# Two-round loops on TensorE in a load-bound decode kernel

## Chip, cores, metric

One core of one Trainium2 chip. The metric is device time in microseconds, the median of several runs; "span" is the time from the first to the last instruction in the profiled run, 1.7 us less than that run's time. Every run quoted as a comparison is fast (on one core: not more than 1.5% above the fastest run of the same kernel), except where it is said.

## The reference, cut to what matters

```python
x  = A_x                                   # 4 x 1 x 512
xn = layernorm(x)
q  = (xn @ wq)                             # 32 heads of 128; 8 KV heads, window of 1024 keys
p  = softmax(q @ k.T / sqrt(128));  o = p @ v
s  = o @ wo                                # wo: 4096 x 512
h  = gelu(layernorm(xn) @ w1 + b1)         # 512 x 1792
g  = silu(h @ w2 + b2)                     # 1792 x 512
return x + s * g
```

All is bfloat16. Four tokens meet 28.85 MB of weights and cache, so each byte is used by very little arithmetic.

## The kernel before

A recording layer keeps the operations of each engine in program order and derives the semaphore waits. Each of the eight K groups (1 MB) is transposed in four tiles of eight matmuls, copied by VectorE, and used for scores; each V group goes into 32 matmuls plus one for the softmax denominators. Everything is written out: 1089 matmuls on TensorE. There are eight 1 MB buffers, so a V load waits for the transposes of the K group whose buffer it takes.

```python
def T(n):                                  # transposes of tile n, then VectorE's copy
    ...
    t = add("pe", fn, d_k[g], c_id, cp.get(n - NB), ...)       # eight pe.transpose into psK
    cp[n] = add("dve", lambda e: e.tensor_copy(kt_buf[:, n % NKT, :], psK[n % NB][:, 0:1024]),
                t, sc.get(n - NKT))
...
for n in range(LAG, NUN + LAG):            # all 8 groups x 4 tiles, LAG = 8
    if n < NUN: T(n)
    S(n - LAG)                             # scores; exp on ScalarE after every fourth
load_v(0); d_w1 = ...; load_v(1); d_w2 = ...
for g in range(HKV):
    if g >= 2: load_v(g)
    if g == 4: d_wox = ...                 # last 128 rows of wo: 60 + 60 + 8 KB, outer dimension 3, 3 and 8
    PV(g)
    if g == 0: epilogue(0); mlp1()
    if g >= 2: epilogue(g - 1)
    if g == 1: mlp2(); mlp3()              # second layer: 56 matmuls of 4 columns, and b2
    if g == 2: mlp4()
epilogue(HKV - 1)
rows = to_rows()                           # all groups, after the last epilogue
wo(... wox ...); wo(... groups 0-6 ...); wo(... group 7 ...)
```

The result is then multiplied by the gate, transposed, added to x and stored.

The softmax here doesn't subtract the row's maximum and nothing guards it: scores larger than these inputs give would overflow.

## Time and profile before

| kernel before | |
|---|---|
| time, median of 3 (range) | 76.81 us (76.61 to 76.92) |
| span | 75.0 us |
| last completion of the last load | 71.89 us |
| packets on TensorE's instruction queue | 8 of 16 KB |

The prediction below shows the lines. One kind of record needs a word: the trace has, for each load, when each of its parts completed. A load over all sixteen DMA engines has sixteen parts (sixteen completion records), and a consumer waits for the last one: the last part of the last load comes at 71.89 us and the four matmuls that read it start at 71.94. The wox loads, with outer dimensions 3, 3 and 8, end in 3, 3 and 8 parts. "The parts" below are always those of the very last load, a quarter of wo's last group, in us from the start of the span. They say how far the sixteen engines had come when the stream of loads ended.

### The profile page before, as it was taken

The page shows a single profiled execution, that of the slowest core. Times are in us where ns is not written, and L with a number is a line of the kernel's source. Part 1 is how long each engine was busy: PE and PEld are TensorE (multiplying, and loading weights), DVE is VectorE, ACT ScalarE, POOL GpSimd, SP SyncE. Part 2 cuts the span into 40 slices and gives each one's busy share as a digit, 9 for nine tenths or more (in the row PEclk, how much of TensorE's full clock was granted, in tenths as well). Part 3 has the DMA queues.
Part 4 walks back from the last instruction along what each step waited for, and adds up shares of the span by engine and source line. Part 5 has one row for each costly group of instructions (what it writes and reads, how often), then busy time and mean ns, then how long its engine had stood idle before and what let it go on. Part 6 is the DMA issues. An engine that isn't in the chain of part 4 may idle for free.

```text
span 75.0 us, 2384 instructions
## 1 busy us (share of the span) xinstructions
PE 49.1 (66%) x1089; PEld 40.3 (54%) x1089; DVE 41.2 (55%) x84; ACT 9.7 (13%) x16; POOL 7.2 (10%) x19
## 2 busy tenths in 40 slices
PE   0000029965689999959979937910899977379670
PEld 0000029953279989959979902500886555268640
DVE  0778106894258989959977060269639774620020
ACT  0611000000270320303203600230000000000000
POOL 6999300000000000000000000000000000000000
PEclk9999999999999999999999995555555555555555
DMA  1999999998999999999999999999999999999800
GB/s 37 271 413 420 417 420 476 437 420 376 433 437 433 415 433 420 424 415 464 419 398 425 461 413 401 424 420 428 419 429 428 420 409 420 417 411 419 322 25 2
DMA packets 4266, 28.99 MB, mean 387 GB/s; under 512 B 508, under 2 KB 648, under 8 KB 1697
## 3 DMA queue, kind: packets, MB, share of 16 engines
q1 hardware_dynamic: 4206, 28.84, 92.6%
q8 instruction: 8, 0.13, 0.6%
q10 hardware_dynamic: 50, 0.01, 0.1%
q14 instruction: 2, 0.01, 0.0%
HBM read 28.85 MB, written 0.00 MB: 385 GB/s over the span
## 4 chain that ended last, share of the span: by engine, by line
DMA 39%; PE 34%; SPq 15%; DVE 5%; issue 3%
DMA wo_sb<-in_A_wo_dram 26%; PE psK L299 20%; SPq L510 14%; DMA kv_buf<-in_A_k_cache_dram 13%; PE psS L318 6%; DVE kt_buf L305 4%; PE psO L383 3%; PE psS L314 2%; PE psM L555 2%; DVE q_sb L389 1%; PE psK L395 1%; PE psK L367 1%; PE psS L576 1%; SPq L218 1%; SPq L211 0%
## 5 line engine op out<-in xcount | busy, mean ns | idle before, releaser
L299 PE MATMUL psK<-ident,kv_buf 128*128 128x128 bf16 x256 | 20.5, 231 | 11.9 <-DMA kv_buf<-in_A_k_cache_dram 10.7
L305 DVE COPY kt_buf<-psK 128x1024 bf16<-128x1024 bf16 x32 | 21.1, 691 | 7.4 <-PE psK L299 7.3
L299 PEld LDWEIGHTS psK<-ident,kv_buf 128*128 128x128 bf16 x256 | 16.3, 104 | 11.3 <-DMA kv_buf<-in_A_k_cache_dram 10.7
L318 PEld LDWEIGHTS psS<-qT,kt_buf 128*128 128x128 bf16 x256 | 9.4, 96 | 2.1 <-issue 1.2
L318 PE MATMUL psS<-qT,kt_buf 128*128 128x16 bf16 x256 | 10.4, 169 | 0.2 <-issue 0.2
L336 PEld LDWEIGHTS psO<-P_buf,kv_buf 128*128 128x128 bf16 x256 | 7.5, 103 | 3.4 <-DMA kv_buf<-in_A_v_cache_dram 1.8
L336 PE MATMUL psO<-P_buf,kv_buf 128*128 128x16 bf16 x256 | 8.0, 174 | 0.9 <-DVE den_sb L349 0.7
L349 DVE TENSOR_REDUCE den_sb<-psS 128x16 f32<-128x512 f32 x8 | 5.5, 687 | 5.1 <-PE psS L342 4.9
L326 ACT ACTIVATE P_buf<-psS 128x512 bf16<-128x512 f32 x8 | 4.8, 597 | 16.2 <-PE psS L318 16.2
L555 PE MATMUL psM<-OW,wo_sb 128*128 128x4 bf16 x124 | 4.1, 167 | 0.8 <-DMA wo_sb<-in_A_wo_dram 0.8
L342 PE MATMUL psS<-P_buf,ones_bf 128*128 128x512 bf16 x8 | 4.5, 561 | 0.0
L555 PEld LDWEIGHTS psM<-OW,wo_sb 128*128 128x128 bf16 x124 | 3.7, 105 | 1.1 <-DMA wo_sb<-in_A_wo_dram 0.9
L572 DVE TENSOR_TENSOR sg_sb<-psM,g_sb 128x16 f32<-128x16 f32 x1 | 0.2, 185 | 5.8 <-PE psM L555 5.8
L421 PE MATMUL psK<-w_sb,yT 128*32 128x448 bf16 x16 | 2.0, 561 | 1.8 <-issue 1.8
L314 PE MATMUL psS<-negm,ind 128*128 128x512 bf16 x8 | 3.0, 380 | 0.0
L449 PE MATMUL psM<-ident,b_sb 4*128 4x16 bf16 x1 | 0.2, 190 | 3.8 <-DVE hT L444 3.8
L431 DVE SCALAR_TENSOR_TENSOR kt_buf<-kt_buf,psK 128x448 f32<-128x448 f32 x1 | 0.6, 622 | 3.7 <-ACT kt_buf L430 3.7
L449 PEld LDWEIGHTS psM<-ident,b_sb 4*128 4x128 bf16 x1 | 0.1, 99 | 4.3 <-DVE hT L444 4.3
L390 ACT ACTIVATE q_sb<-psO 128x512 bf16<-128x512 f32 x1 | 0.6, 597 | 13.1 <-PE psO L383 13.1
L267 DVE CAST P_buf<-x_bf 4x512 f32<-4x512 bf16 x1 | 1.0, 956 | 2.2 <-DMA x_bf<-in_A_x_dram 2.2
L352 DVE RECIPROCAL rden<-den_sb 128x16 f32<-128x16 f32 x8 | 2.0, 253 | 0.3
L440 DVE TENSOR_TENSOR kt_buf<-kt_buf,psK 128x448 bf16<-128x448 f32 x1 | 2.1, 2083 | 0.0
(74 smaller groups left out, 36.0 us busy)
## 6 DMA issues: line engine op xcount, KB each, us to landing
kv_buf<-in_A_k_cache_dram SPq DMA_DIRECT2D x8, 1024.0 KB, 20.6
kv_buf<-in_A_v_cache_dram SPq DMA_DIRECT2D x8, 1024.0 KB, 24.0
wq_sb<-in_A_wq_dram SPq DMA_DIRECT2D x2, 2048.0 KB, 11.4
w_sb<-in_B_w_dram SPq DMA_DIRECT2D x2, 1792.0 KB, 28.3
wo_sb<-in_A_wo_dram SPq DMA_DIRECT2D x3, 1024.0 KB, 24.0
wo_sb<-in_A_wo_dram SPq DMA_DIRECT2D x1, 512.0 KB, 19.6
wo_sb<-in_A_wo_dram SPq DMA_DIRECT2D x1, 256.0 KB, 16.4
wo_sb<-in_A_wo_dram SPq DMA_DIRECT2D x1, 128.0 KB, 14.6
```

The lines of the kernel that those rows point to most:

```text
L299: last = pe.transpose(psK[n % NB][:, j * 128:(j + 1) * 128], kv_buf[:, g, u * UT + j, :], ident[:, :])
L305: cp[n] = add("dve", lambda e: e.tensor_copy(kt_buf[:, n % NKT, :], psK[n % NB][:, 0:1024]), t, sc.get(n - NKT))
L314: pe.matmul(psS[g % 2][:, 0:512], ind[:, :], negm[:, :], start=True, stop=False, skip_group_check=True)
L318: last = pe.matmul(psS[g % 2][:, c * 16:(c + 1) * 16], kt_buf[:, n % NKT, j * 128:(j + 1) * 128], qT[:, g * 16:(g + 1) * 16], start=False, ...
L326: ex[g] = add("act", lambda e: e.activation(P_buf[:, g, :], psS[g % 2][:, 0:512], AF.Exp, scale=SCALE), sc[n])
L336: last = pe.matmul(pso[:, 0:16], kv_buf[:, (HKV + g) % NS, c, :], P_buf[:, g, c * 16:(c + 1) * 16], start=(c == 0), stop=(c == NC - 1))
L342: den[g] = add("pe", lambda pe: pe.matmul(psS[g % 2][:, 0:512], ones_bf[:, :], P_buf[:, g, :], start=True, stop=True), ex[HKV - 2 + g % 2] ...
L349: v = add("dve", lambda e: e.tensor_reduce(den_sb[:, cs], bass.AP(psS[g % 2], 0, [[512, 128], [1, 16], [16, NC]]), AX.X, ALU.add), den[g])
L383: last = pe.matmul(psO[m // 4][32 * s:32 * s + 32, 0:512], xT[:, c, :], wq_sb[:, c, m * 512:(m + 1) * 512], start=(c == 0), stop=(c == 3), ...
L440: v = add("dve", lambda e: e.tensor_tensor(bass.AP(kt_buf, 4 * UT * 128, [[NKT * UT * 128, 128], [1, 32], [32, FC]]), f32k(3).rearrange("p ...
L510: d_wo.append((g0, g1, i0, i1, pg.dma("sp", "wo%d" % n, lambda e: e.dma_start(wo_sb[:, g0:g1, i0:i1, :], wo_r[:, g0:g1, i0:i1, :]))))
L555: last = pe.matmul(psM[:, PS_W + c * 4:PS_W + (c + 1) * 4], w[:, c * 128:(c + 1) * 128], o, start=(st and c == 0), stop=sp, skip_group_che ...
```

## The change

Its intent is to halve TensorE's program: K groups 0-3 and 4-7 run through the same instructions, and so do V groups 0-3 and 4-7. For that, both rounds must name the same buffers (hence qR, the one tile from which both rounds read their queries, and the copies of P, the softmax weights), semaphores are lowered again in the loop, and the second MLP layer stands in a branch taken in the first V round only, in a form with fewer instructions. The rows of groups 0 to 6 are made ahead of the last epilogue, and wox, the load of the last 128 rows of wo, becomes two loads with outer dimensions 5 and 3. The queries are now made before the first transposes, and the scores follow the transposes by 3 tiles and no longer by 8. Cut to its core:

```diff
     def emit_pe(self, pe):
+                with pe.Fori(0, 2, 1) as i:
+                    ...                    # all operations of the first round, waits valid for both
+                    if first:
+                        with pe.If(i < 1):
+                            ...            # the second MLP layer
+                    for name, (s, step) in mine.items():
+                        pe.sem_inc(s, -step)
...
-    d_wq = [load_wq(0)]; load_k(0); load_k(1); d_wq.append(load_wq(1)); load_k(2..7)
+    d_wq = [load_wq(0), load_wq(1)]; load_k(0..3)
...
-            kv_buf[:, (HKV + g) % NS, :, :], ...), t_last[(HKV + g) % NS]
+            kv_buf[:, NG + g % NG, :, :], ...), pv_op[g - NG] if g >= NG else None
...
+        if g < NG:
+            pc[lg] = add("act", lambda e: e.activation(
+                P_buf[:, lg, :], P_buf[:, NG + lg, :], AF.Copy), den[g], cls="pc")
...
     def mlp3():
-            for k in range(FC):
-                for c in range(4):
-                    last = pe.matmul(psM[:, PS_Z + c * 4:PS_Z + (c + 1) * 4],
-                                     w2_sb[:, k, c * 128:(c + 1) * 128], hT[:, k, 0:4], ...)
+            for k in range(FC):
+                i, m = k % 4, 32 if k < 4 else 4
+                last = pe.matmul(psK[1][32 * i:32 * i + m, 0:1024].bitcast(F32), hT[:, k, 0:m],
+                                 w2_sb[:, k, :], ..., tile_position=(0, 32 * i))
...                                           # then a copy, and 4 matmuls that fold the four parts
+    d_wox = [... for p0, n, b0 in ((0, 5, 0), (32, 3, 80))]    # 16 KB per engine and load
...
         PV(g)
+        if g == HKV - 1:
+            row_w = rows_first()              # groups 0-6
+        epilogue(g)
```

## The prediction

> **What bounds the kernel now.** I read the page first, slices before sums.
>
> ```profile
> span 75.0 us, 2384 instructions
> ...
> PE 49.1 (66%) x1089; PEld 40.3 (54%) x1089; DVE 41.2 (55%) x84; ACT 9.7 (13%) x16; POOL 7.2 (10%) x19
> ...
> PEclk9999999999999999999999995555555555555555
> DMA  1999999998999999999999999999999999999800
> GB/s 37 271 413 420 417 420 476 437 420 376 433 437 433 415 433 420 424 415 464 419 398 425 461 413 401 424 420 428 419 429 428 420 409 420 417 411 419 322 25 2
> ```
>
> No engine is busy over two thirds of the span, but the DMA row stands at 8 or 9 from slice 2 to slice 37, at some 420 GB/s. 28.85 MB read from HBM at 0.42 MB/us is 68.7 us; with a ramp of some 2 us that is the whole time up to 71 us. So the stream of loads is the bound, provided nothing else is late at its end. That is the second view, TensorE's timeline at the end:
>
> ```profile
> 69.73 1.01 PE L555 MATMUL psM<-OW,wo_sb 128*128 128x4 bf16 x32 [0.54 <-DMA wo_sb<-in_A_wo_dram]
> 70.98 1.23 PE L555 MATMUL psM<-OW,wo_sb 128*128 128x4 bf16 x28 [0.23 <-DMA wo_sb<-in_A_wo_dram]
> 72.48 0.38 PE L576 MATMUL psS<-ident,sg_sb 128*16 128x128 f32 x1 [0.28 <-DVE sg_sb L572]
> ```
>
> Before both of the last wo groups TensorE waits for the load (0.54 and 0.23 us). It is early, but by under a microsecond. After the last load come 12 matmuls, a multiply, a transpose, an add and the store: about 3 us that the change leaves alone.
>
> Third, is TensorE itself held up by anything that loops would change?
>
> ```profile
> q8 instruction: 8, 0.13, 0.6%
> ```
> ```profile
> 26.60 0.29 PE L318 MATMUL psS<-qT,kt_buf 128*128 128x16 bf16 x6 [0.16 <-issue]
> 33.08 0.22 PE L299 MATMUL psK<-ident,kv_buf 128*128 128x128 bf16 x1 [0.81 <-issue]
> 39.09 0.38 PE L299 MATMUL psK<-ident,kv_buf 128*128 128x128 bf16 x4 [0.42 <-issue]
> 45.48 1.68 PE L421 MATMUL psK<-w_sb,yT 128*32 128x448 bf16 x15 [1.81 <-issue]
> ```
>
> The four waits on "issue" lie 127 matmuls (254 instructions) apart each. The trace's packet records have eight 16384-byte packets on that queue, ending at 25.2, 31.7, 37.8 and 44.0 us for the first four; TensorE resumes 1.3 to 1.5 us after each. The fourth started 4.0 us after TensorE had crossed the boundary before it. [...] TensorE stalls 3.2 us in all. These stalls are not on the path that ends the kernel, because TensorE still waits for wo.
>
> The fetch also hurts the loads a little. The records of the sixteen completions of each load lie within 0.5 us for every load up to the first fetch; after it one part is 1.2 us behind, after the fourth four are, and at the last load eleven parts come 0.5 to 1.6 us after the earliest (70.25 to 71.89 us). Three of these carry the two 60 KB wox loads, which complete in three parts only. Perfect balance would end at the mean of the sixteen, 71.29: 0.6 us is all that balance can give.
>
> [...]
>
> **The change, part by part.**
> *Bytes and order.* The same 28.85 MB. The order becomes wq, k0-3, w1, k4-7, v0-3, w2, wox, v4-7, wo. At 0.42 MB/us from before's ramp (estimates): wq at 13, k3 at 23, w1 at 27, k7 at 37, v3 at 47, w2 at 52, v7 at 62, last wo at 71-72. No gain, unless a buffer is late.
> *Buffers.* k4-7 now wait for the transposes of k0-3, v4-7 for the PV of v0-3. K round 0 is limited by arrivals and ends near 27; k4 is released near 18, while the queue holds work until 27. v0-3 have free buffers. v4 must be issued by about 50; PV(0) follows round 1 (k7 at 37 plus four tiles of 0.69 us, 40) and mlp1 (2 us), so 43.5. Slack 6 us.
> *Instructions.* TensorE's program falls from 1089 to 649 matmuls, two instructions each. With waits and branches I count about 1345 instead of 2200: fetches fall from eight to about five if looped pages stay in memory. In that case the stalls of 3.2 us nearly vanish, off the path. The K body is 530 instructions, just over two pages, and touches three; the V body with the second layer touches three as well.
> *Second MLP layer.* 57 matmuls (1.65 us) become 14 wide ones in four column groups plus 5: at the halved clock about 4 rounds of 0.43 us (512 columns; estimate from mlp1, 15 matmuls in 1.68 us), then a 0.6 us copy on ACT and 0.5 us: 3 us serial, starting when w2 lands at 52, done at 55. v4 lands at 54.5, so V round 1 keeps pace with the loads: PV(7) at 62.3, as before.
> *Rows.* The 16 matmuls for groups 0-6 (0.30 us) now run beside epilogue 7 (1.1 us). wo 0-1 starts with its load at 64.7 and no longer at 67.3. About 1.3 us more slack at the tail, on a path that waits for wo anyway: worth nothing.
> *wox and fetch balance.* The three engines carry 32 KB, not 40 KB (8 KB at 26 GB/s: 0.3 us), and three fetches fewer are 48 KB over 16 engines (0.1 us). Together the last load lands 0.1 to 0.4 us sooner.
> *Added, off the path.* Four P copies on ACT at 0.6 us; ACT is 13% busy. One qR copy. Two branches taken.
> Sum: 76.8 minus 0.1 to 0.4, so 76.5.
>
> **The rivals.**
> *The branch back misses*[...]. Each branch back then waits about 6.4 us and the rounds refetch three pages. K round 1 starts at 33 instead of 30 and ends near 45; PV(0) ends near 49 and v4 is barely in time. The branch of V at 58 costs until 64.5, the second half ends near 71 and wo would run behind its loads: about 82 us, and up to 90 if the second page is asked for only on entering the first. [...] Against: [...] a layout cut to two rounds over three pages makes sense only if pages stay.
> *A gap in the loads*, from four buffers each for K and V where K had eight. SyncE waits for TensorE now too (18.1 us behind S in the waits of SyncE's queue) and the DMA row shows no hole, because loads are issued 16 to 24 us ahead of their landing (medians of the list of issues). A gap needs PV(0) after 50 us: plus 1 to 3 us.
> *The stalls were the bound after all* and removing them gives 2 to 3 us. Against: TensorE's waits for wo at the very end. The floor is balanced loads without any fetch, near 75.7.
>
> **Range and chances.** Pages kept, about three in four: 75.9 to 77.0. Pages lost or a gap, under one in four: 78 to 90. The floor of 75.7 is short of the 75.3 that 2% needs, so faster has little. I predict 76.5 us, range 75.6 to 78.3; faster 0.05, same 0.76, slower 0.19. The range leaves the refetch case out, which I know.
>
> **What would show it.** Right: the DMA row stays at 9 from slice 2 to 37; about five packets on the instruction queue; no issue wait over 1 us where K round 1 starts (28 to 34 us) or where V round 1 starts (55 to 62); TensorE waits for wo before the last groups; last completions within 1.3 us of each other. Wrong: ten or more instruction packets with a wait of 4 us or more at the first tile of a second round; a hole in the DMA row near 50 us; or wo matmuls that run without a DMA wait at the end, which makes TensorE the bound. A fall under 75.3 would mean that the fetch costs the loads more than their lag shows.

Passages are cut from this text where it is marked. The sum came to 76.8 minus 0.1 to 0.4, so 76.5 us; its 26 GB/s is an estimate from 420 GB/s over sixteen engines. The trace of before has no branch back, so "about three in four" and the up to 90 us of the rival stand as estimates. The 6.4 us of that rival is the time from 39.09 us, where TensorE resumes after its third wait on issue, to 45.48, where it resumes after the fourth; that a page is asked for only when TensorE crosses the boundary before it was an assumption. In the second MLP layer, 0.43 us a round is about a quarter of mlp1's 1.68 us, and the 0.5 us of the five matmuls was a guess.

## The result

The changed kernel takes 76.72 us (76.64 to 76.81, 4 runs; before 76.81 in the same rounds). The ratio is 0.9992 with a 95% interval of 0.9968 to 1.0016: no difference. Ratios here and below are the mean time of one kernel's fast runs over that of the other's of the same rounds, so not quite the ratio of the medians quoted. The page of the changed kernel, the same rows as the prediction shows of before:

```profile
span 75.0 us, 2351 instructions
...
PE 51.5 (69%) x1045; PEld 41.3 (55%) x1045; DVE 40.6 (54%) x85; ACT 12.5 (17%) x21; POOL 8.5 (11%) x24
...
PEclk9999999999999999999999999855555555555555
DMA  0999999999999989999999999999999999999700
GB/s 20 262 419 422 430 445 402 420 428 437 419 475 391 466 380 415 432 424 428 424 432 432 415 419 473 401 420 422 424 424 419 419 413 426 421 421 417 277 13 2
...
q8 instruction: 5, 0.08, 0.4%
```

The DMA row has no hole and the rate is the same. TensorE executes nearly as many matmuls as before (1045: both rounds count), but five pages were fetched for it and no longer eight. TensorE's timeline at the places that the prediction named:

```profile
31.42 2.01 PE L398 MATMUL psK<-ident,kv_buf 128*128 128x128 bf16 x32 [1.37 <-PEq L101]
...
52.73 1.89 PE L563 MATMUL psK<-w_sb,hT 128*32 128x512 bf16 x14 [2.58 <-DMA w_sb<-in_B_w_dram]
55.31 0.19 PE L572 MATMUL psM<-ident,b_sb 4*128 4x16 bf16 x1 [0.69 <-ACT kt_buf L568]
55.44 1.87 PE L576 MATMUL psM<-fold,kt_buf 128*128 128x4 f32 x8
57.16 1.00 PE L437 MATMUL psO<-P_buf,kv_buf 128*128 128x16 bf16 x32
...
62.61 1.00 PE L437 MATMUL psO<-P_buf,kv_buf 128*128 128x16 bf16 x32 [0.99 <-PEq L101]
...
64.82 1.02 PE L692 MATMUL psM<-OW,wo_sb 128*128 128x4 bf16 x32 [0.55 <-DMA wo_sb<-in_A_wo_dram]
...
69.80 1.01 PE L692 MATMUL psM<-OW,wo_sb 128*128 128x4 bf16 x32 [1.49 <-DMA wo_sb<-in_A_wo_dram]
71.04 1.24 PE L692 MATMUL psM<-OW,wo_sb 128*128 128x4 bf16 x28 [0.23 <-DMA wo_sb<-in_A_wo_dram]
```

At 31.42 the second K round starts. The wait ahead of it is put down to TensorE's own sequencer, because both rounds of a load share a semaphore that TensorE lowers; the completion records say what it was: the last part of K group 4 came at 31.28, while fourteen of its parts had come by 29.63. TensorE shows no wait for a fetch of its own there, nor at 57.16, where the second V round begins. At the end TensorE waits for wo as before, only longer (1.49 us).

The sixteen parts of the last load complete from 70.39 to 71.97 us; before, from 70.25 to 71.89. More than 1.0 us after the earliest came ten parts before and come eight now. The last is as late as it was, and so is the kernel.

### The profile page after: what moved, and what is told of

It reads as the page before. It is cut to its first block, busy times and chain, and to the rows that moved or that the text cites. A ratio compares the mean times of both kernels' runs of the same rounds, so it can differ in the third digit from the quotient of the medians.

```text
span 75.0 us, 2351 instructions
## 1 busy us (share of the span) xinstructions
PE 51.5 (69%) x1045; PEld 41.3 (55%) x1045; DVE 40.6 (54%) x85; ACT 12.5 (17%) x21; POOL 8.5 (11%) x24
## 4 chain that ended last, share of the span: by engine, by line
PE 22%; DMA 22%; SPq 6%; DVE 3%; ACT 2%; issue 1%
DMA wo_sb<-in_A_wo_dram 22%; PE psK L398 10%; SPq L676 6%; PE psS L418 4%; PE psO L437 2%; PE psK L529 1%; PE psS L444 1%; PE psS L414 1%; DVE kt_buf L539 1%; DVE den_sb L454 1%; PE psM L692 1%; ACT P_buf L426 1%; ACT kt_buf L538 1%; PE psS L714 1%; PE psK L533 0%
## 5 line engine op out<-in xcount | busy, mean ns | idle before, releaser
L418 PE MATMUL psS<-qR,kt_buf 128*128 128x16 bf16 x256 | 10.6, 170 | 0.0
L418 PEld LDWEIGHTS psS<-qR,kt_buf 128*128 128x128 bf16 x256 | 9.7, 97 | 1.3 <-issue 0.3
L486 PE MATMUL psO<-wq_sb,xT 128*32 128x512 bf16 x32 | 3.8, 627 | 2.9 <-DMA wq_sb<-in_A_wq_dram 2.7
L492 DVE CAST q_sb<-psO 128x512 bf16<-128x512 f32 x1 | 0.7, 691 | 6.5 <-PE psO L486 6.5
L563 PE MATMUL psK<-w_sb,hT 128*4 128x512 bf16 (+1 forms) x14 | 1.9, 623 | 2.6 <-DMA w_sb<-in_B_w_dram 2.6
L486 PEld LDWEIGHTS psO<-wq_sb,xT 128*32 128x32 bf16 x32 | 0.9, 128 | 5.0 <-DMA wq_sb<-in_A_wq_dram 3.6
L448 ACT ACTIVATE P_buf<-P_buf 128x512 bf16<-128x512 bf16 x4 | 2.4, 621 | 1.6 <-PE psS L444 1.6
L563 PEld LDWEIGHTS psK<-w_sb,hT 128*4 128x4 bf16 (+1 forms) x14 | 0.6, 107 | 3.4 <-DVE rden L457 3.1
## 6 DMA issues: line engine op xcount, KB each, us to landing
kv_buf<-in_A_k_cache_dram SPq DMA_DIRECT2D x8, 1024.0 KB, 12.4
```

Of the source, the lines that this page charges most:

```text
L418: last = pe.matmul(psS[lg % 2][:, c * 16:(c + 1) * 16], kt_buf[:, n % NKT, j * 128:(j + 1) * 128], qR[:, lg * 16:(lg + 1) * 16], start=Fal ...
L486: last = pe.matmul(psO[m // 4][32 * s:32 * s + 32, 0:512], xT[:, c, :], wq_sb[:, c, m * 512:(m + 1) * 512], start=(c == 0), stop=(c == 3), ...
L563: last = pe.matmul(psK[1][32 * i:32 * i + m, 0:1024].bitcast(F32), hT[:, k, 0:m], w2_sb[:, k, :], start=(k < 4), stop=(k >= FC - 4), tile_ ...
```

## The experiments

The main theory going in: a load is complete when its slowest part is; a fetched page puts the engine that carries it behind (one part by 1.2 us after the first fetch in the trace of before); how many engines are behind makes no difference, so fewer fetches gain nothing, and TensorE's saved stalls lie beside the loads. The rivals: fetches cost in proportion to their bytes; or the loops gained and another part of the change gave it back.

### Loops written out (e1_unrolled)

```diff
-                with pe.Fori(0, 2, 1) as i:
+                for i in range(2):
...
-                        with pe.If(i < 1):
-                            for op in first: ...
+                    if first and i == 0:
+                        for op in first: ...
```

> The changed kernel with both loops written out (the same instructions in the same order, no branch). Main theory: a load is complete when the slowest of its sixteen parts is, and one fetched page puts one part about 1.2 us behind; whether four or eight parts are late makes no difference to the last. So: 8 or 9 packets on the instruction queue instead of 5, waits on issue of 2 to 4 us in TensorE's timeline, last completion of the last wo load at 71.8 to 72.2 us (71.97 with loops), time 76.5 to 77.0. Rival (the fetches cost the loads in proportion to their bytes): 0.06 us each, so +0.2 us. Rival (the loops did gain, and another part of the change gave it back): slower by 0.4 us or more, 77.1 or above.

Measured: 76.73 us (76.53 to 76.92), ratio to before 0.9995 (0.9979 to 1.0012). Two groups of its waits, and its instruction queue:

```profile
PE psS L443 <- issue: 2.0, 1, 2.0
...
PE psM L691 <- issue: 0.6, 1, 0.6
```
```profile
q8 instruction: 8, 0.13, 0.6%
```

Eight pages, the waits on issue are back, eleven parts are more than 1.0 us late and not eight, and the last of them comes at 71.87 us. The loops alone are worth nothing that these runs can resolve (0.15 us or so), and nothing else in the change hid a gain of theirs.

### wo's last group over all engines (e2_plain7)

```diff
-    d_wox = [...]                          # loads over 5 and 3 engines
-    w3_r = A_wo[7 * 512:7 * 512 + 384, :] ...
+    wo_sb[:, 7, i0:i1, :] <- wo_r[:, 7, i0:i1, :]   for (0, 3), (3, 4)
...                                         # rows of group 7 by the same selection as groups 0-6
```

> The changed kernel with the last group of wo loaded and turned like the other seven, over all sixteen DMA engines: the loads on 5 and 3 engines are gone, the same bytes. Main theory: the parts made late by a fetch stay 1.1 to 1.2 us behind, the others gain 8 KB (0.3 us), so the last completion comes at 71.6 to 71.9 and the time is 76.4 to 76.7, hardly better. Rival (the loads on few engines alone set the last part): last completion 71.3 or earlier, time 76.1 or less.

Measured: 76.93 us, ratio 1.0024 (1.0011 to 1.0037), a little slower than the kernel before. The parts run from 70.33 to 72.12. Eleven lie within 0.45 us of the first, one is 1.06 behind, four are 1.6 to 1.8 behind. By 70 us the trace has four 16 KB instruction packets for TensorE and one of 8 KB on the other instruction queue: the late parts are exactly as many. They also appear one by one: without the part behind the 8 KB packet, one is late in w1, after the first packet, two in K group 4, after the second, three in w2, after the third, and four in the last load. So each of TensorE's packets made another part late and none the same one twice, which is why eight need not cost more than four. The late parts are 1.4 to 1.6 us behind the middle of the eleven, though a packet took 0.9 us (0.88 to 0.97 us in the traces of before and after). My number had the wrong sign, however. A likely reason, not tested by itself: spreading 128 KB over sixteen engines gives each 8 KB more, the delayed ones too, so the loads on few engines were a compensation that took 0.3 us of work (an estimate from 420 GB/s over 16) off the eleven engines that they left alone.

### wox on 8 and on 2 engines (e6_wox8, e7_wox2)

```diff
-    for p0, n, b0 in ((0, 5, 0), (32, 3, 80))
+    for p0, n, b0 in ((0, 8, 0),)          # e7_wox2: (0, 2, 0), 16 rows each
```

> The changed kernel with the 128 KB of wox on 8 engines, 16 KB each, in one load; it had 32 KB on three engines and 16 KB on two. The run without wox showed the parts behind a fetch 1.4 to 1.7 us behind at the end, later than any wox part (0.9 to 1.2 us expected for 32 KB). Theory (the parts behind a fetch are the last): the wox parts come sooner, the last completion does not: 71.8 to 72.1 us, time within 0.2 us of 76.7. It can be up to 0.6 us later if a fetch falls on one of the 8 engines. Rival (the wox parts are the last, as the prediction's 0.3 us assumed): last completion 71.4 to 71.6, time 76.2 to 76.4.

Measured: 77.28 us (76.73 to 77.48), ratio 1.0038 (1.0006 to 1.007). Six runs in two clumps: 76.73 and 76.86, and four from 77.24 to 77.48. In the profiled run, one of the second clump, the last completion is at 72.43, two parts standing 0.4 us behind all others. The records do not name engines, but they tell which these are: five of the eight wox parts completed at 51.15 to 51.55 and one at 52.39, while two came at 52.92 and 52.93, as only an engine behind one of TensorE's fetches does (in the load just before, the three parts behind them came at 52.30 to 52.33, all others by 51.78). So two engines carried a fetch and 16 KB of wox. That the other clump is the case without such a meeting was not looked at, for want of a profile. The rival, which wanted 76.2 to 76.4, is out.

> The same 128 KB on 2 engines, 64 KB each: 2.4 us more than the engines without them at 26 GB/s (an estimate from 420 GB/s over 16), so now these two must be the last. Theory (slowest part sets the end): last completion 72.6 to 73.1 us with two parts alone at the end, time 77.4 to 77.9. Rival (bytes count in total only): no change, 76.7.

Measured: 78.88 us, ratio 1.0264 (1.0245 to 1.0283), 2.0 us more than the kernel before in the same rounds (76.87). The parts end at 72.62 for all but two, then 73.53 and 74.05: two parts alone, as expected, and 2.4 to 3.0 us behind the middle of the parts that are not late (2.4 expected). But all are later than expected, so the time missed the range by 1 us. The first part comes at 71.03 instead of 70.39 too, and the rate falls to 272 GB/s in one slice near 53 us. Why two overloaded engines also hold up the others was not settled.

### Instruction packets on an idle engine (e3_fetch_gp)

```diff
             pg.emit("gp", gp)
+            for n in range(640):
+                gp.sem_inc(pad_sem, 1 - 2 * (n % 2))
```

> The changed kernel with 640 instructions that do nothing of use (a semaphore up and down) at the end of GpSimd's queue, which is otherwise idle from 11 us: more instruction packets beside the same loads, and TensorE untouched. Theory (slowest part): if these packets fall on one engine, five of 16 KB put one part 4 to 6 us behind and the time goes to 79 or more; if they rotate over engines, each part is delayed by 1 us at most and the time stays within 0.5 us of 76.7, up to 77.8 if one engine gets two. Rival (costs in proportion to bytes): 80 KB are 0.2 us in either case.

Measured: 79.28 us, ratio 1.0321 (1.0301 to 1.034).

```profile
q8 instruction: 5, 0.08, 0.4%
q14 instruction: 6, 0.05, 0.1%
```

The other instruction queue has six packets of 8 KB; the changed kernel has one there (the second of the two on its page has 88 bytes). So five are new. Fifteen parts end at 71.97 or sooner, the same as without them; one ends at 74.44, 4.1 us behind the middle of the eight earliest. So all the extra packets hit one DMA engine, and 40 KB, 0.14% of the bytes, cost 2.4 us (79.28 against 76.87 for the kernel before in the same rounds). In proportion to bytes it would have been 0.1 us (40 KB at 420 GB/s). This is the cleanest sign that the slowest engine is the bound. The size has luck in it, however: one part of each wox load is late as well (53.76 and 54.36, the others by 52.52), so the engine that was hit also carries the 32 KB of wox. That is 1.2 us of its 4.1 (an estimate from 420 GB/s over 16), which leaves about 0.6 us for each 8 KB packet, itself 0.3 us long (0.31 us in the traces of before and after).

### All pages fetched at the start (e4_warm, e5_warm_plain7)

```diff
+        with pe.Fori(0, 2, 1) as o:
+            for group in (("pre", "k"), ("mid", "v"), ("post",)):
+                with pe.If(o > 0):
                     ...                    # everything as before
```

In the first round of this outer loop TensorE only branches through its pages. e5_warm_plain7 has e2_plain7's edit as well.

> The changed kernel inside one more loop of two rounds whose first round branches over all work, through pages 2, 4 and 5 and back, while TensorE has nothing to do (it is idle until 7.9 us). Since pages stay once fetched, all fetches should come in the first 8 us and none after. Main theory: the parts on few engines (32 KB, 1.2 us) are still late, so the last completion moves by 0.4 us at most and the time is 76.3 to 76.8. Rival (fetches alone set the end): last completion near 71.0, time 75.8. If branching far costs too much, TensorE starts after 8 us, but it waits for wq until 13 us, so that costs nothing. If pages do not stay: as many packets again later.

> Both edits together: no fetch while the loads run at their full rate, and no load on few engines. Main theory (the slowest part sets the end): only now no part is late; the sixteen completions of the last load lie within 0.6 us as they do at the start, the last at 70.8 to 71.2, time 75.6 to 76.0, clearly more than the sum of the two single edits. Rival (costs add in proportion to bytes): no more than the sum of the two, 76.4 or above. Rival (TensorE is the bound at the end by now): its wo matmuls run without a wait for a load and the time stays at 76.5.

Measured: 84.55 us (82.43 to 86.13) and 85.14 us (82.42 to 85.92). Five of six runs of each are slow, so only the one fast run of each, 82.43 and 82.42, is compared; neither carries more than "far slower". The profiled runs are slow ones, so their times are not compared either. The page and the start of TensorE's timeline of e4_warm:

```profile
DMA  4799999999996100789999999999999999999900
...
q8 instruction: 5, 0.08, 0.5%
```
```profile
23.44 0.26 PE L480 MATMUL psS<-ident,xn_bf 4*128 4x4 bf16 x4 [23.44 <-issue]
```

The walk took 23 us, not 8: packets start at 5.8, 12.2, 12.4 and 20.3 us, with gaps of 6.4 and 7.9 us, and a last one at 25.9, when the work has begun. So pages asked for beside the loads seem to come one after another, as TensorE reaches each. TensorE starts at 23.4, buffers stay full, and the DMA row has a hole. As a remedy it failed. As a measurement it is clear: all five pages were fetched by 27 us, and then no packet for TensorE came until the end, although both loops branched back. Here no looped page was fetched twice. In e5_warm_plain7 no part of the last load is 1.0 us late (78.11 to 79.04), but the hole may have let engines catch up, so this does not show what an undisturbed stream without fetches would reach.

### The remaining parts of the change (e8_rows_after, e9_mlp_narrow)

```diff
-        if g == HKV - 1:
-            row_w = rows_first()
         epilogue(g)
+        if g == HKV - 1:
+            row_w = rows_first()           # waits for the last epilogue
```

> The changed kernel with the rows of groups 0 to 6 made after the last epilogue again, as before the change. Prediction's claim: worth nothing, because TensorE waits for wo anyway: the first wo matmuls start near 66.6 us and no longer at 64.8, the wait ahead of the third wo load shrinks from 1.49 us to about 0, and the time stays at 76.7 +- 0.2. Rival (the move paid for something that the loops cost): slower by 0.4 us or more.

Measured: 76.59 us, ratio 0.9969 (0.9953 to 0.9986). TensorE's timeline:

```profile
65.95 0.99 PE L692 MATMUL psM<-OW,wo_sb 128*128 128x4 bf16 x32 [0.49 <-DVE OW L632]
...
69.58 1.01 PE L692 MATMUL psM<-OW,wo_sb 128*128 128x4 bf16 x32 [0.27 <-DMA wo_sb<-in_A_wo_dram]
```

The first wo matmuls start 1.1 us later, and the wait ahead of the third load shrinks from 1.49 to 0.27 us. The time even fell a little, which asked for a repeat beside the unedited change.

> The changed kernel unedited, to have it beside the next two on one chip. 76.5 to 76.9 us, ratio to the kernel before 0.997 to 1.002.

> The run with the rows after the last epilogue again (0.9969 of the kernel before, which is 0.2 us less than the unedited change at 0.9992, but not from the same rounds). If moving the rows ahead costs something real, it is again 0.2 us below the unedited change of these rounds. If the difference was one of rounds and of where the fetches fell, the two lie within 0.1 us of each other, since TensorE waits for the last loads in both.

> The changed kernel with the second MLP layer as before the change (57 matmuls of 4 columns, one after the other into one tile), still between the V halves. In the trace of the change the wide form took TensorE from 52.7 to 57.2 us, 4.4 us and not the 3 of the prediction; the narrow one took 1.65 us, so the second V half should start at about 54.6 and no later than its load at 55. Theory (all of this lies beside the loads): time as the unedited change within 0.15 us. Rival (the 2 us by which the second half starts late are what the loops gained elsewhere): faster by 0.3 us or more.

```diff
     def mlp3():
-            ...                            # 14 wide matmuls, a copy, 5 that fold and add b2
+            ...                            # 56 narrow matmuls and b2, as before the change
```

Measured in the same rounds: the unedited change 76.66 us, ratio 0.9982 (0.9963 to 1.0002); rows after the epilogue 76.75, ratio 0.999 (0.9972 to 1.0009); narrow second layer 76.72, ratio 0.9984 (0.9965 to 1.0004). The three lie within 0.1 us. The 0.2 us of the first try did not come back; what made it is not known (the tries were on different chips). The narrow layer's timeline:

```profile
52.52 1.79 PE L562 MATMUL psM<-hT,w_sb 128*128 128x4 bf16 x56
55.09 1.00 PE L437 MATMUL psO<-P_buf,kv_buf 128*128 128x16 bf16 x32 [0.79 <-PEq L101]
```

With it the second V half starts at 55.1, two microseconds sooner than with the wide form, and it does not matter: the loads come no sooner.

### One sum over all runs

| kernel | last completion, us | span, us | difference |
|---|---|---|---|
| before | 71.89 | 74.97 | 3.08 |
| changed | 71.97 | 75.05 | 3.08 |
| e1_unrolled | 71.87 | 74.95 | 3.08 |
| e2_plain7 | 72.12 | 75.21 | 3.09 |
| e3_fetch_gp | 74.44 | 77.52 | 3.09 |
| e4_warm (slow run) | 81.32 | 84.41 | 3.09 |
| e5_warm_plain7 (slow run) | 79.04 | 82.13 | 3.09 |
| e6_wox8 | 72.43 | 75.51 | 3.08 |
| e7_wox2 | 74.05 | 77.14 | 3.09 |
| e8_rows_after | 71.71 | 74.80 | 3.09 |
| after_again (unedited) | 71.81 | 74.89 | 3.08 |
| e8_again | 71.86 | 74.95 | 3.09 |
| e9_mlp_narrow | 72.06 | 75.15 | 3.09 |

Whatever was edited, the span ends 3.08 to 3.09 us after the last part of the last load. That is the whole of TensorE's, VectorE's and the store's share of the path. No edit gave a gain over both kernels that came back in a second try. The six comparisons that leave the loads as the change has them (changed twice, e1, e8 twice, e9) all have ratios just under 1, 0.9985 in the mean: a gain of some 0.1 us over the kernel before is possible, but e1 has it without loops.

## Why the prediction was right, and where a step was off

- **The stream of loads is the bound, the tail fixed.** Right: the table above.
- **Looped pages are not fetched again** (taken as three in four). Right: five packets as counted, no wait for a fetch at either branch back. The rival of the missed branch did not happen; in e4_warm five packets come as well, and none after 27 us.
- **TensorE's 3.2 us of issue stalls are off the path.** Right: e1_unrolled has such stalls (2.0 and 0.6 us) and the same time (76.73 us).
- **No gap in the loads from fewer buffers.** Right: the DMA row stays at 8 or 9 from slice 2 to 37. Two times were off, without effect. Round 0 of K ended near 30 us, not 27: it was not limited by arrivals, as the last part of K group 3 had come at 22.90 and TensorE waits for no load between 16.65 and 30.04; it started when the queries were done, and its first 32 transposes took 3.6 us where the same 32 in the second round took 2.0. And PV(0) came at 45.0, not 43.5, inside the slack of 6 us.
- **Second MLP layer: "3 us serial ... done at 55".** Mis-sized: from 52.73 to 57.16 us, 4.4 us. The term that was too small is the "5 matmuls, 0.5 us": in float32 they show as eight matmuls of 1.87 us. V round 1 started 2 us late and caught up by PV(7) (62.61 against the 62.3 foreseen). e9_mlp_narrow shows that it costs nothing.
- **Rows ahead are worth nothing.** Right: e8_again and the unedited change are 0.1 us apart, and the slack (1.3 us foreseen) appeared as a wait 1.2 us longer (1.49 against 0.27).
- **"Together the last load lands 0.1 to 0.4 us sooner."** This step failed. It landed 0.08 us later in the first trace (71.97 against 71.89) and 0.08 sooner in the repeat (71.81). The 0.3 us assumed that the three wox engines alone were the last. In the trace of before they were level with others: their parts completed at 54.67 to 54.87, and five parts of the load just before, behind a fetch, at 54.48 to 54.85. Lightening the three leaves those five where they are, and e2_plain7, with no wox engine at all, still ends at 72.12. The 0.1 us averaged three fetches over sixteen engines, although the span ends 3.08 to 3.09 us after the slowest part in every run of the table. Four fetches or eight, the last part is one fetch behind, because each fell on another part: in the trace of before the loads after TensorE's first to seventh packets have 1, 2, 3, 5, 6, 10 and 11 late parts, with one more from the fourth on after the 8 KB packet at 39.9 us of the other instruction queue, and three more from the sixth on after wox. In place of 76.5 the sum is then 76.8 minus nothing; measured 76.72 and 76.66. That 76.5 came close to the measured time is no merit of this step; without it the sum would have been closer.
- **"The last completions within 1.3 us of each other".** Wrong for the same reason: 1.58 us.
- **Readings of the trace of before.** Three were loose, without effect on the sum. The eleven late parts of the last load come 0.8 to 1.6 us after the earliest, not 0.5 to 1.6. The load after the fourth packet has five late parts (46.70 to 47.56 us, the others by 46.11), not four; four is the load before it. The medians from issue to landing of the large loads run from 11.4 to 28.3 us, not from 16 to 24. That three of the eleven are engines of wox fits the records: in the load just before wox six parts are late (54.00 to 54.85 us, the others by 53.51), in the one just after it nine (56.46 to 57.34, the others by 55.95). The "some 420 GB/s" is a mean: the full slices run from 376 to 476 with a mean of 423.

Open: how a fetch whose packet takes 0.9 us puts its engine 1.4 to 1.6 us behind; which engines the packets fall on, and why TensorE's fall on one after another but GpSimd's all on one; and what a stream without any fetch would take, since no experiment got the pages in ahead of the loads for free.

## What to carry to other kernels

In a kernel bound by loads over sixteen engines, ask which engine finishes last, not how many bytes there are: 40 KB of instruction fetches on one engine, which also carried 32 KB of wox, cost 2.4 us here, while three pages of TensorE's fetches fewer gained nothing, because other pages still made parts late. An edit that speeds up an engine which waits for loads at the end only turns into a longer wait there (1.49 us against 0.27 for the rows made ahead); read that wait before and after to see the slack move. The two-round loops on TensorE cost no time that could be measured (76.72 us with them, 76.73 written out), with a program of which five pages were fetched; here they bought only a shorter program, and a much longer one was not tried.
